# Reordering the loads of a two-problem attention kernel: fifth chunk's tokens earlier, weight blocks at a shorter lead, the second problem's tokens sooner

## The chip, the cores and the metric

One core of a Trainium2 chip. The metric is device time in microseconds (us) of one execution.

## The reference

Two independent problems, A and B, of the same shape; each is a grouped-query attention block with cached keys and values, and the two outputs are put side by side.

```python
B, Sq, D = 16, 32, 1024                # x: 512 tokens of 1024, bf16
Hq, Hkv, Sk, Dh = 32, 4, 512, 128      # 32 heads on 4 cached key/value heads
q = (x @ wq)                           # wq: 1024 x 4096
scores = einsum("bhqd,bhkd->bhqk", q, k) * Dh ** -0.5
p = softmax(scores)
o = einsum("bhqk,bhkd->bhqd", p, v)
out = o.reshape(B, Sq, Hq * Dh) @ wo   # wo: 4096 x 1024
# result: concatenate([A's out, B's out], axis=-1)
```

## The kernel before

The tokens of a problem are needed with the model dimension on the partitions, in eight chunks of 128 ("token chunks" below). A's first four chunks are transposed on TensorE, the others by transposing DMAs. The projection of A's first eight heads is done chunk by chunk (`first_heads`), with the weights in eight pieces (`load_w0`). Everything later is a software pipeline of 128 slots, one for each pair of batch and key/value head: a slot does four matmuls of 256 columns for scores, four for values, and seven matmuls of 512 columns (six in every fourth slot) out of one long stream: the remaining heads of A's projection, B's projection, A's output, B's output.

```python
# start: order of the loads, all issued by SyncE [cut: tokens and weights of the first four chunks]
load_w0(0, HC, NF, REP)              # HC = 4
load_w0(HC, HC + 2, 0, REP)          # weights of chunks 4 and 5, 512 KB
load_x_transposed(HC)                # tokens of chunks 4 and 5
load_w0(HC + 2, DC, 0, REP)          # weights of chunks 6 and 7
load_x_transposed(HC + 2)            # tokens of chunks 6 and 7
load_wq(0, 2)                        # third weight block (heads 8 to 11), 1 MB
load_k(0); load_wq(0, 3); load_k(1); load_v(0); load_k(2); load_wq(0, 4); load_v(1)
# ... [cut]
first_heads(range(NF, REP), range(HC))
first_heads(range(REP), range(HC, DC - 2))    # chunks 4, 5: the first that need DMA-transposed tokens
# ... [cut: chunks 6, 7, and the copies out of PSUM]

def stream():                                 # [cut: output projections]
    for h in range(REP, HQ):
        yield from q_units(0, h)              # eight matmuls of 512 columns per head
    for h in range(HQ):
        yield from q_units(1, h)

units = stream()
run(units, 5)

plan = {}
def at(slot, fn, *args):
    plan.setdefault(slot, []).append((fn, args))

for j in range(2, 2 * NG // GRP):             # NG = 64, GRP = 4
    if j > 2:
        at(GRP * (j - 1) - 2, load_k, j)      # four transposing DMAs for A, one for B
    at(GRP * (j - 1) + 2, load_v, j, 2 if j < 3 else 1)
for c4 in range(5, 16):                       # weight blocks of four heads, 1 MB each
    need = (c4 - 2) * 4 * DC / 7.0
    at(max(0, int(need) - 10), load_wq, c4 // 8, c4 % 8)
for n, (d0, d1) in enumerate(((0, 2), (2, 5), (5, DC))):
    at(GRP * (n + 4) - 2, load_xT_b, d0, d1)  # B's tokens, transposing DMAs
# ... [cut: output weights]

for i in range(total_slots + LAG):
    if live:
        do_loads(i)
        scores(i)
    run(units, 1)
    # ... [cut: sums, values(i - LAG), normalize]
    run(units, 5)
    # ...
    run(units, 1 - (i % 4 == 3))
```

`do_loads(i)` does not tie a load to the time of slot `i`. It puts the load into SyncE's instruction list at that place; SyncE works through the list in order. In the trace of before, B's last tokens, put at slot 22, whose scores began at 70.5 us, were issued at 79.7; and the waits of SyncE that its view shows up to 110 us, after 0.7 us at the start, are 3.1 us, all for TensorE to free buffers. So a slot number is a place in a queue.

A caution on names: the block of heads 8 to 11 is called the third weight block (`c4` = 2, counted from one), but "fifth" to "ninth" weight block are `c4` = 5 to 9 of the loop, counted from zero. `c4` = 8 is B's first block.

## Time and profile before

| | before |
|---|---|
| time, median of the first three runs | 343.88 us (343.65 to 345.03) |
| span of the profiled execution (344.67 us) | 342.9 us |
| TensorE listed busy | 338.1 us |
| seven 512-column and eight 256-column matmuls (one slot), start to start | 2.38 us |
| granted TensorE clock, mean | 1.000 |

The page of the kernel before: busy time of the engines with the share of the span, and the chain of waits that ended last by engine.

```profile
PE 338.1 (99%) x2128; PEld 214.3 (63%) x2128; DVE 266.4 (78%) x336; ACT 186.1 (54%) x209; POOL 47.0 (14%) x206
...
PE 92%; DMA 4%; SPq 3%; issue 0%; ACT 0%; ACTq 0%
```

Listed busy time of TensorE says little, since matmuls overlap in this trace: a 512-column matmul is listed with 379 ns, but seven of them start within 1.51 us, 216 ns apart. So the question is whether the starts are ever further apart than that. The timeline of TensorE of the kernel before (start, length, instruction, count, and in brackets the idle time before it and who ended it):

```profile
7.60 5.17 PE L532 MATMUL q_ps<-xT,w_sb 128*128 128x512 bf16 x22
13.34 7.07 PE L532 MATMUL q_ps<-xT,w_sb 128*128 128x512 bf16 x32 [0.57 <-DMA xT<-in_A_x_dram]
...
85.47 0.59 PE L302 MATMUL q_ps<-xT,wq_sb 128*128 128x512 bf16 x2
86.22 1.02 PE L302 MATMUL q_ps<-xT,wq_sb 128*128 128x512 bf16 x4 [0.16 <-DMA xT<-in_B_x_dram]
```

There are two gaps in brackets: the first projection waits for the tokens of chunks 4 and 5, and B's projection, five matmuls in, waits for B's last tokens. The chain of waits shows when these DMAs were issued (start, length):

```profile
5.85 7.45 DMA xT<-in_A_x_dram
13.34 7.07 PE q_ps L532 x32
...
79.71 6.47 DMA xT<-in_B_x_dram
86.22 1.02 PE q_ps L302 x4
```

One more number matters for the argument: the third weight block, the first that the stream needs. Its DMA in the view of the weight tile, to 13 us:

```profile
L246 SPq DMA_DIRECT2D wq_sb<-in_A_wq_dram x1: 582/582/582, 12.3 to 12.3; - x1
...
DMA to landing us min/median/max: 7.7/7.7/7.7
```

It was issued at 12.3 and landed at 20.0 us. The stream's first matmul started at 20.24. Landing times below are computed in this way, as issue plus time to landing. By the packed traces of before and of the changed kernel, the 167 DMAs that SyncE issued landed in the order of their issue, in both.

### The profile page before, as it was taken

What the parts mean: (1) busy time and instruction counts of PE and PEld (TensorE: products, weight loads), DVE (VectorE), ACT (ScalarE), POOL (GpSimd) and SP (SyncE); (2) the same over time, 40 slices, a digit from 0 to 9 for tenths busy, and PEclk for the clock granted to TensorE, in tenths of its full rate; (3) what the DMA queues carried; (4) which work ended last, traced back from release to release, by engine and by line L of the source; (5) the groups of instructions that cost most, each with busy time, mean ns of one, the idle gap of its engine ahead of it and who ended that gap; (6) DMA issues with size and microseconds to landing.
All of it is one profiled execution on the core that took longest, in us unless ns stands there. A gap on an engine that the chain in (4) does not pass through costs nothing.

```text
span 342.9 us, 5510 instructions
## 1 busy us (share of the span) xinstructions
PE 338.1 (99%) x2128; PEld 214.3 (63%) x2128; DVE 266.4 (78%) x336; ACT 186.1 (54%) x209; POOL 47.0 (14%) x206
## 2 busy tenths in 40 slices
PE   8999999999999999999999999999999999999996
PEld 7356666666666666666666666666666666666555
DVE  1057988888888888988888889888988888888540
ACT  3067666666676666766655455555455455555010
POOL 0001111100111111111101212221122110111100
PEclk9999999999999999999999999999999999999999
DMA  6998999999999999989999557998449996530001
GB/s 177 284 229 185 353 244 277 234 188 231 248 280 276 267 261 232 228 243 280 269 332 289 138 124 190 273 331 221 118 118 298 337 188 139 113 103 0 17 17 33
DMA packets 127086, 71.70 MB, mean 209 GB/s; under 512 B 75857, under 2 KB 126289, under 8 KB 127057
## 3 DMA queue, kind: packets, MB, share of 16 engines
q1 hardware_dynamic: 126528, 70.21, 85.4%
q0 software_dynamic: 384, 1.05, 0.9%
q8 instruction: 17, 0.28, 0.4%
q14 instruction: 13, 0.10, 0.1%
q10 hardware_dynamic: 144, 0.07, 0.1%
HBM read 50.86 MB, written 2.10 MB: 154 GB/s over the span
## 4 chain that ended last, share of the span: by engine, by line
PE 92%; DMA 4%; SPq 3%; issue 0%; ACT 0%; ACTq 0%
PE f_ps L321 32%; PE q_ps L302 26%; PE s_ps L358 16%; PE ob L426 16%; DMA xT<-in_A_x_dram 2%; PE q_ps L532 2%; DMA xT<-in_B_x_dram 2%; SPq L276 1%; SPq L478 1%; SPq L466 0%; SPq L246 0%; ACT o_sb L330 0%; SPq L287 0%; SPq L705 0%; ACTq L330 0%
## 5 line engine op out<-in xcount | busy, mean ns | idle before, releaser
L366 ACT ACTIVATE p_sb<-s_ps,shift 128x1024 bf16<-128x1024 f32 x128 | 142.7, 1115 | 100.0 <-PE s_ps L358 87.5
L377 DVE TRANSPOSE_TENSOR_REDUCE parts<-p_sb 128x32 f32<-128x1024 bf16 x128 | 158.9, 1241 | 19.8 <-ACT p_sb L366 18.3
L321 PE MATMUL f_ps<-wo_sb,oT 128*128 128x512 bf16 (+1 forms) x544 | 131.8, 366 | 0.0
L302 PE MATMUL q_ps<-xT,wq_sb 128*128 128x512 bf16 x448 | 117.7, 379 | 0.2 <-DMA xT<-in_B_x_dram 0.2
L426 PE MATMUL ob<-p_sb,v_sb 128*128 128x256 bf16 x512 | 76.8, 273 | 0.0
L358 PE MATMUL s_ps<-qT,kT 128*128 128x256 bf16 x512 | 76.8, 273 | 0.0
L321 PEld LDWEIGHTS <-oT 128*128 128x128 bf16 x544 | 53.2, 98 | 36.0
L358 PEld LDWEIGHTS <-kT 128*128 128x128 bf16 x512 | 56.8, 113 | 28.4 <-issue 0.3
L302 PEld LDWEIGHTS <-wq_sb 128*128 128x128 bf16 x448 | 43.8, 98 | 31.9 <-issue 0.4
L426 PEld LDWEIGHTS <-v_sb 128*128 128x128 bf16 x512 | 50.1, 98 | 20.0
L448 DVE TENSOR_TENSOR oT<-r,ob 128x512 bf16<-128x512 f32 x64 | 44.0, 688 | 22.5 <-PE ob L426 22.0
L412 DVE STREAM_TRANSPOSE r<-rall 128x512 f32<-128x512 f32 x64 | 44.3, 691 | 1.1
L310 ACT CAST qT<-q_ps 128x512 bf16<-128x512 f32 x56 | 32.7, 583 | 14.1 <-PE q_ps L302 14.1
L395 POOL COPY half<-cs 64x32 f32<-64x32 f32 x32 | 6.6, 206 | 228.7 <-DVE cs L385 228.7
L330 ACT CAST o_sb<-f_ps 128x512 bf16<-128x512 f32 (+1 forms) x17 | 9.5, 559 | 24.4 <-PE f_ps L321 16.7
L532 PE MATMUL q_ps<-xT,w_sb 128*128 128x512 bf16 (+1 forms) x70 | 15.2, 368 | 0.6 <-DMA xT<-in_A_x_dram 0.6
L385 DVE TENSOR_REDUCE cs<-parts 128x32 f32<-128x128 f32 x32 | 12.0, 376 | 1.1
L532 PEld LDWEIGHTS <-w_sb 128*128 128x128 bf16 x70 | 6.8, 100 | 7.8 <-issue 0.9
L407 DVE RECIPROCAL rall<-sums 128x32 f32<-128x32 f32 x32 | 10.4, 325 | 1.6 <-POOL sums L404 1.6
L560 DVE CAST qT<-q_ps 128x512 bf16<-128x512 f32 x4 | 2.8, 692 | 10.4 <-PE q_ps L532 10.3
L332 POOL DMA_DIRECT2D out_dram<-o_sb x8 | 4.6, 575 | 33.1 <-ACT o_sb L330 33.1
L396 POOL TENSOR_TENSOR half<-half,cs 64x32 f32<-64x32 f32 x32 | 7.8, 244 | 2.6
(25 smaller groups left out, 47.0 us busy)
## 6 DMA issues: line engine op xcount, KB each, us to landing
wq_sb<-in_B_wq_dram SPq DMA_DIRECT2D x8, 1024.0 KB, 6.0
wo_sb<-in_A_wo_dram SPq DMA_DIRECT2D x8, 1024.0 KB, 6.3
v_sb<-in_B_v_cache_dram SPq DMA_DIRECT2D x16, 512.0 KB, 4.4
wo_sb<-in_B_wo_dram SPq DMA_DIRECT2D x8, 1024.0 KB, 8.1
v_sb<-in_A_v_cache_dram SPq DMA_DIRECT2D x15, 512.0 KB, 6.4
wq_sb<-in_A_wq_dram SPq DMA_DIRECT2D x6, 1024.0 KB, 6.1
w_sb<-in_A_wq_dram SPq DMA_DIRECT2D x2, 512.0 KB, 7.0
kT<-in_A_k_cache_dram SPq DMA_TRANSPOSE x64, 4.5
```

What stands on the lines that cost most here:

```text
L302: nc.tensor.matmul(ps[:], lhsT=w[:, dc, (h % 4) * DH:(h % 4 + 1) * DH], rhs=xT[pr][:, dc, :], start=(dc == 0), stop=(dc == DC - 1),)
L310: nc.scalar.copy(out=qT[pr, g][:, :, hl, :], in_=ps[:].rearrange("p (b s) -> p b s", s=SQ),)
L321: nc.tensor.matmul(ps[:, 0:width], lhsT=oT[pr, tt][:, h, :], rhs=wo_tiles[pr, nh, h // REP][:, h % REP, off:off + width], start=(h == 0), ...
L358: nc.tensor.matmul(s_ps[:, c, :], lhsT=kT[:, i % GRP, c, :], rhs=qT[pr, g][:, b, :, :].rearrange("p h s -> p (h s)"), start=True, stop=True,)
L366: nc.scalar.activation(out=p_sb[:], in_=s_ps[:], func=ACTF.Exp, bias=shift[:], scale=SCALE)
L377: nc.vector.tensor_reduce(out=parts[k][:, q, :, :].rearrange("p c h -> p (c h)"), in_=st[i]["p"][:].rearrange("p c (h s) -> p (c h) s", s=SQ),
L385: nc.vector.tensor_reduce(out=cs[:], in_=parts.pop(k)[:].rearrange("p q c h -> p q h c"), axis=AX.X, op=ALU.add,)
L407: nc.vector.reciprocal(out=rall[:, k, :], in_=quad.pop(k)[:])
L412: nc.vector.transpose(out=r[:].rearrange("p n s -> p (n s)"), in_=rall[:, k, o * 2 * REP:(o + 1) * 2 * REP] .unsqueeze(2).to_broadcast([P, ...
L426: nc.tensor.matmul(ob[j][:, q, :], lhsT=v_sb[:, i % GRP, c, :], rhs=st[i]["p"][:, c, :], start=(c == 0), stop=(c == KC - 1),)
L448: nc.vector.tensor_tensor(out=out, in0=rcp.pop(j)[:].rearrange("p (q h) s -> p q h s", h=REP), in1=ob.pop(j)[:].rearrange("p q (h s) -> p ...
L532: nc.tensor.matmul(first_q[h][:, ts], lhsT=w0[dc // HC][:, dc % HC, h * DH:(h + 1) * DH], rhs=xT[0][:, dc, ts], start=(dc == 0 and t0 == 0 ...
```

## The change

The intent: tokens of chunks 4 and 5 should not queue behind the weights of chunk 5; weight blocks should not push the keys, values and B's tokens back by arriving long before they are needed; B's tokens should come sooner. The rate of the stream in the formula is corrected to 6.75 matmuls a slot. A split adds a DMA, and loading the third values in one piece removes one.

```diff
-            load_w0(HC, HC + 2, 0, REP)
+            load_w0(HC, HC + 1, 0, REP)
             load_x_transposed(HC)
+            load_w0(HC + 1, HC + 2, 0, REP)
             load_w0(HC + 2, DC, 0, REP)
@@
-                at(GRP * (j - 1) + 2, load_v, j, 2 if j < 3 else 1)
+                at(GRP * (j - 1) + 2, load_v, j)
             for c4 in range(5, 16):
-                need = (c4 - 2) * 4 * DC / 7.0
-                at(max(0, int(need) - 10), load_wq, c4 // 8, c4 % 8)
+                need = ((c4 - 2) * 4 * DC - 5) / 6.75
+                at(max(0, int(need) - 7), load_wq, c4 // 8, c4 % 8)
@@
-                at(GRP * (n + 4) - 2, load_xT_b, d0, d1)
+                at(GRP * (n + 3) - 2, load_xT_b, d0, d1)
```

(The diff is cut; the rest of it is `load_v` without its pieces.)

More of the change, by code (lines that the diff above doesn't have):

```diff
@@ L280, in load_k, with load_v @@
                     )
-            def load_v(j, pieces=1):
+            def load_v(j):
                 v_sb = v_tiles[j] = kv.tile([P, GRP, KC, DH], BF16, name="v_sb")
-                v = kv_part(j, 2).rearrange("q (p c) d -> p q c d", c=KC)
-                for k in range(pieces):
-                    qs = slice(k * GRP // pieces, (k + 1) * GRP // pieces)
-                    nc.sync.dma_start(out=v_sb[:, qs], in_=v[:, qs])
+                nc.sync.dma_start(
+                    out=v_sb[:],
+                    in_=kv_part(j, 2).rearrange("q (p c) d -> p q c d", c=KC),
+                )
             xT = [None, None]
```

## The prediction

> **What bounds it now.** TensorE: the busy table gives PE 338.1 of 342.9 us, the chain of waits is 92% PE, granted clock 1.00. Busy time is a poor witness, as matmuls overlap ([...]here a 512-column matmul is listed with 379 ns), so I use the pitch of starts: in the timeline seven 512-column matmuls take 1.51 us (0.216 each), four 256-column ones 0.44; one slot (seven and eight of these) is 2.38 us, and from 20 us on slots follow at that pitch. The chain shows two places where data is missed after the first blocks:
> 1. 13.34 us: the first projection waits for transposed tokens of chunks 4 and 5 (idle 0.57 us; in pitch about 0.7). Issued at 5.85, landed 13.25, behind 512 KB of weights of chunks 4 and 5.
> 2. 86.22 us: B's sixth token chunk, issued at 79.71, landed 86.2 (idle 0.16; in pitch about 0.3).
>
> **What the change does.** No instruction on PE, DVE or ACT changes, only the order on SyncE's DMA queue. One weight load is split in two, one values load merged.
> - Tokens 4/5 have 256 KB less ahead. [...] At the 300 GB/s of 8 to 10 us (windows) that is 0.85 us (estimate): landing near 12.4, so wait 1 shrinks below 0.2. Chunk 5's weights land near 13.3, needed 14.4.
> - But the gain meets the next load: the third weight block, issued at 12.31, landed at 20.0, and its first weights entered PE at 20.04. DMA is saturated from 5 to 20 us and the bytes ahead of that block are unchanged, so it lands at 20.0 again; PE arrives near 19.6 and waits 0.3 to 0.5. Net gain at the start: 0 to 0.3 us.
> - B's tokens, four slots (9.5 us) sooner: the last part lands near 77 to 79, needed 85.9. Wait 2 vanishes: 0.3 us.
> - Weight blocks: seven slots' lead (16.7 us) against 6 us (up to 10.2) from issue to landing. Estimated landing against need, from the queue's pace (7.3 us per A chunk): fifth block 47 to 48 against 50.8 (before: 43.2); sixth 57 to 60 against 61.2 (before 50.7); seventh 66 against 72.5; B's first 78 against 83.7. The sixth is tightest. No stall expected.
> - After about 110 us the queue waits for buffers PE frees, so nothing changes to the end.
>
> **Prediction.** 343.88 - 0.3 - 0.1 = about 343.5 us; 8 in 10: 342.7 to 344.4 (before's three runs alone spread 1.4 us). Faster by over 2%: 0.01; within 2%: 0.97; slower by over 2%: 0.02.
>
> **What would show each step.** Token transposes landing about 12.4, PE's gap before chunk 4 under 0.2 us; a new gap of about 0.4 us at 20 us before the first matmul of the streamed projection, for its weight block; no wait for B's tokens near 86; the sixth weight block landing before 61 us without a wait; the same pitch and tail (13.7 us of output matmuls) afterwards.
>
> **What would make it wrong.** That weight block landing before 20.0, so that the start gains the full 0.6; the DMA queue slower in 40 to 60 us, so that the fifth or sixth block comes late and PE stalls; or transposes next to weights behaving otherwise than bytes over rate.

## The result, and the profile after

| | before | changed |
|---|---|---|
| time, median of 6 runs each | 344.77 us (343.65 to 345.5) | 343.89 us (343.45 to 344.2) |
| ratio, 95% interval | | 0.9977 (0.9955 to 0.9999) |
| span of the profile | 342.9 us | 342.3 us |

Executions over 1.5% slower than the fastest of the same kernel are left out of the means. A ratio here is the mean time of one kernel's fast runs over that of the other's fast runs of the same rounds, so it is not quite the ratio of the medians. The time lies inside the predicted range, and the change is "the same" at 2%.

The page of the changed kernel:

```profile
PE 337.9 (99%) x2128; PEld 214.1 (63%) x2128; DVE 266.2 (78%) x336; ACT 185.9 (54%) x209; POOL 46.7 (14%) x206
...
PE 96%; DMA 1%; SPq 1%; ACT 0%; issue 0%; ACTq 0%
```

The timeline of TensorE of the changed kernel, and below it that of the weight loads into TensorE:

```profile
7.63 12.12 PE L533 MATMUL q_ps<-xT,w_sb 128*128 128x512 bf16 x54
19.97 1.25 PE L302 MATMUL q_ps<-xT,wq_sb 128*128 128x512 bf16 x5 [0.21 <-ACT qT L561]
...
85.21 1.46 PE L302 MATMUL q_ps<-xT,wq_sb 128*128 128x512 bf16 x6
```

```profile
8.35 10.91 PEld L533 LDWEIGHTS <-w_sb 128*128 128x128 bf16 x52 [0.62 <-DMA w_sb<-in_A_wq_dram]
19.96 0.76 PEld L302 LDWEIGHTS <-wq_sb 128*128 128x128 bf16 x5 [0.71 <-DMA wq_sb<-in_A_wq_dram]
```

Both gaps of before are gone: nothing waits for tokens in the first projection, and B's projection runs through at 85 us. (The 54 matmuls take 12.12 us where other profiles have 11.84: one waits 0.29 us at 8.35, for weights.) A new wait stands at 20 us: the weights of the stream's first matmul go in at 19.96, when the third weight block has landed. The 0.71 us in that row are idle time of the weight loads, which otherwise run ahead (in this packed trace a load starts 0.11 us before its matmul in the median, this one 0.004 us); of TensorE's own time 0.38 us are lost (its starts there are 0.59 us apart instead of 0.22). Its DMA:

```profile
L246 SPq DMA_DIRECT2D wq_sb<-in_A_wq_dram x1: 581/581/581, 10.6 to 10.6; - x1
...
DMA to landing us min/median/max: 9.4/9.4/9.4
```

It was issued 1.7 us sooner than before and landed at practically the same time, 20.0 (to the hundredth, 19.92 for 19.99). The tokens of chunks 4 and 5 landed at 11.4 for 13.3. B's last tokens landed at 72.6 (issued at 68.7) for 86.2. The fifth, sixth and seventh weight blocks landed at 47.3, 57.0 and 67.1, later than before (43.2, 50.7, 58.2), as predicted, and nothing waited for them.

So far the picture is the one that was predicted. But it is made of one profiled execution of each kernel, and a gap of 0.3 us in one profile need not be there in the next. The experiments therefore had to answer two things: which part of the change does what, and how steady the two gaps of before are.

### The profile page after: what moved, and what is told of

Its sections match the earlier page's. It is cut to its first block, busy times and chain, and to the rows that moved or that the text cites. A ratio compares the mean times of both kernels' runs of the same rounds, so it can differ in the third digit from the quotient of the medians.

```text
span 342.3 us, 5511 instructions
## 1 busy us (share of the span) xinstructions
PE 337.9 (99%) x2128; PEld 214.1 (63%) x2128; DVE 266.2 (78%) x336; ACT 185.9 (54%) x209; POOL 46.7 (14%) x206
## 4 chain that ended last, share of the span: by engine, by line
PE 96%; DMA 1%; SPq 1%; ACT 0%; issue 0%; ACTq 0%
PE f_ps L321 32%; PE q_ps L302 28%; PE ob L426 16%; PE s_ps L358 16%; PE q_ps L533 3%; DMA w_sb<-in_A_wq_dram 1%; SPq L478 0%; SPq L466 0%; ACT qT L561 0%; ACT o_sb L330 0%; SPq L706 0%; ACTq L330 0%
## 5 line engine op out<-in xcount | busy, mean ns | idle before, releaser
L377 DVE TRANSPOSE_TENSOR_REDUCE parts<-p_sb 128x32 f32<-128x1024 bf16 x128 | 158.8, 1241 | 20.0 <-ACT p_sb L366 18.3
```

The source lines that it names most:

```text
L377: nc.vector.tensor_reduce(out=parts[k][:, q, :, :].rearrange("p c h -> p (c h)"), in_=st[i]["p"][:].rearrange("p c (h s) -> p (c h) s", s=SQ),
```

## The experiments

All runs gave correct results. To compare profiles I cut the span into three: until the first matmul of the scores in slot 0 ("first scores"); from there to the start of the last copy out of PSUM ("the slots"); and from there to the end of the span ("the end"). Where nothing waits, the middle part came out as 318.23 or 318.24 us in nine profiles of seven different kernels, so that whatever it has above that is waiting. (Times in us, read from the timelines; "end" uses the span to the hundredth, from the packed trace; "wait" names what the timeline of TensorE shows after first scores.)

| profile | first scores | slots | end | span | wait in the slots |
|---|---|---|---|---|---|
| before | 21.32 | 318.55 | 3.01 | 342.9 | B's tokens |
| before, again (e8) | 20.98 | 318.23 | 3.02 | 342.2 | none |
| before, again (f4) | 20.45 | 320.22 | 3.01 | 343.7 | B's tokens |
| changed | 21.05 | 318.24 | 3.01 | 342.3 | none |
| changed, again (f1) | 20.27 | 318.23 | 3.01 | 341.5 | none |
| e1, start alone | 21.07 | 318.23 | 3.44 | 342.7 | none |
| e2, tokens alone | 21.00 | 318.23 | 3.01 | 342.2 | none |
| e3, lead alone | 20.91 | 318.23 | 3.08 | 342.2 | none |
| f2, changed without start | 20.79 | 318.23 | 3.07 | 342.1 | none |
| e4, half block | 20.79 | 319.06 | 3.44 | 343.3 | values |
| e7 and f3, interleaved | 20.29, 20.72 | 318.23, 318.23 | 3.44, 3.44 | 342.0, 342.4 | none |
| e5, lead of four | 20.78 | 319.70 | 3.01 | 343.5 | weights, B's keys |
| e6, tokens later | 20.41 | 329.74 | 3.01 | 353.2 | B's tokens |

### The parts one at a time: e1, e2, e3 (five rounds, one call)

e1, the kernel before with the reorder of the start only:

```diff
-            load_w0(HC, HC + 2, 0, REP)
+            load_w0(HC, HC + 1, 0, REP)
             load_x_transposed(HC)
+            load_w0(HC + 1, HC + 2, 0, REP)
```

> The kernel before with only the start reordered (fifth chunk's weights and tokens ahead of the sixth's weights). My theory: the 0.57 us wait of the first projection at 13.3 us is gone, the third weight block still lands near 20.0, so the weight load at 20 us waits about 0.7 us and the first scores start at 21.05 instead of 21.32: gain 0.25 to 0.3 us. B's tokens are still late: the PE idle of about 0.1 to 0.3 us near 86 us stays or grows by the 0.3 us that PE comes earlier, so that the net gain at the end is about 0, 0 to 0.3 us. Rival (the start alone carries the whole gain): 0.6 us or more at the end, no wait at 86.

Measured: 344.3 us, ratio 1.0000 (0.9985 to 1.0014). First scores at 21.07, as expected, and no matmul of the first projection waited. But the expected wait of 0.7 us at 20 us was not there either: TensorE itself came late in this execution (its long row of 512-column matmuls began at 8.32 us, for 7.60 in before; why, see e7 and f3). And B's last tokens, which this kernel loads as before does, landed at 84.5, and nothing waited near 86. This was the first sign that the gaps of before differ between executions.

e2, the kernel before with B's tokens four slots sooner only:

```diff
-                at(GRP * (n + 4) - 2, load_xT_b, d0, d1)
+                at(GRP * (n + 3) - 2, load_xT_b, d0, d1)
```

> The kernel before with only B's tokens asked for four slots sooner. My theory: no wait for B's tokens near 86 us, last part landing before 80; the wait of 0.57 us at 13.3 stays; gain 0.2 to 0.4 us over before. Rival (tokens sooner push weight blocks back into a new wait): a new PE wait between 45 and 100 us.

Measured: 343.84 us, ratio 0.9988 (0.9973 to 1.0002). B's last tokens landed at 77.4; no wait in the slots; the wait of 0.56 us for the tokens of chunks 4 and 5 stayed. And yet the first scores came at 21.00, no later than with the start reordered (21.05 and 21.07). The rival (a new wait) fell.

e3, the kernel before with the shorter lead (and the values in one piece) only:

```diff
-                need = (c4 - 2) * 4 * DC / 7.0
-                at(max(0, int(need) - 10), load_wq, c4 // 8, c4 % 8)
+                need = ((c4 - 2) * 4 * DC - 5) / 6.75
+                at(max(0, int(need) - 7), load_wq, c4 // 8, c4 % 8)
```

> The kernel before with only the weight blocks' lead (seven instead of ten, and the values load in one piece). My theory: the ninth weight block now stands behind the last part of B's tokens in the queue, not ahead of it, so that this alone also moves those tokens about 3 to 4 us sooner and the wait near 86 us is gone without their being asked for sooner: gain 0.2 to 0.4 us; weight blocks land later but no wait. The two changes are then each sufficient for that wait. Rival (the later blocks cost something): PE waits for a weight block between 45 and 100 us, time equal or worse than before.

Measured: 343.9 us, ratio 0.9993 (0.9979 to 1.0006). B's last tokens were issued at 74.6 and landed at 80.2, although they were not asked for sooner: the ninth weight block (1 MB) had stood ahead of them in the queue and now stood behind. No wait in the slots. So either part alone takes that wait away; in the changed kernel it is taken away twice. (The merge of the third values, which e3 holds too, was not run by itself; it saves one DMA, against the 1 MB block.)

### What binds the start after the change: e4

The changed kernel with the third weight block in two halves:

```diff
-            load_wq(0, 2)
+            load_wq(0, 2, parts=((0, 2), (2, 4)))
```

> The changed kernel with the third weight block loaded in two halves, first two heads first. My theory: after the change the start is bounded by that block's landing at 20.0 us; with the half of it landing near 18.8 the first streamed matmul starts near 19.6 to 19.7 instead of 19.97, first scores near 20.7 to 20.8, gain 0.3 us over the changed kernel unless the first keys (landing 20.4) bind. Rival (what binds at 19.97 is the copy of the seventh head out of PSUM, which ended at 19.95): the first streamed matmul stays at 19.97 and nothing is gained.

Measured: 344.6 us, ratio to before 1.0009 (0.9996 to 1.0023). The first half landed at 17.2. The stream's first matmul started at 19.48 instead of 19.97, right behind the first projection. The rival fell: the copy of ScalarE that the bracket in the changed kernel's timeline names ran here from 19.25 to 19.83 us, and the matmul did not wait for it. So in the profile of the changed kernel it had been the weight block; the bracket names what ended last by the profile, and there the copy (19.36 to 19.94) ended within some hundredths of a microsecond of the landing. But there was no gain. The timelines of TensorE, of the weight loads, and of TensorE again, of this run:

```profile
19.48 1.24 PE L302 MATMUL q_ps<-xT,wq_sb 128*128 128x512 bf16 x5
```

```profile
20.79 0.36 PEld L358 LDWEIGHTS <-kT 128*128 128x128 bf16 x4 [0.56 <-DMA kT<-in_A_k_cache_dram]
```

```profile
31.79 0.61 PE L426 MATMUL ob<-p_sb,v_sb 128*128 128x256 bf16 x4 [0.63 <-DMA v_sb<-in_A_v_cache_dram]
```

The second half's issue took SyncE 3.0 us instead of 0.58, the keys landed at 20.7 for 20.4, and the first values at 31.7 for 30.0, too late. Of the 0.49 us at 19.48, 0.26 were left at first scores, and 0.83 were lost at 31. The end, too, is 0.43 us longer than in the changed kernel, for a reason that has nothing to do with the block (last section on e7 and f3).

### How much room the shorter lead leaves: e5

```diff
-                at(max(0, int(need) - 7), load_wq, c4 // 8, c4 % 8)
+                at(max(0, int(need) - 4), load_wq, c4 // 8, c4 % 8)
```

> The changed kernel with weight blocks at four slots' lead instead of seven. My theory: the lead in slots acts only through the order of the SyncE queue, which runs late in the first 80 us; with four, the sixth block stands behind the fifth values and sixth keys, issues near 57 us, lands near 63, needed at 60.9: PE stalls about 2 us there, and perhaps 0 to 1.5 us more for the seventh. Total 2 to 4 us slower than the changed kernel (346 to 348). Rival (seven slots leave ample spare time, so four does too): no stall, 344.

Measured (3 rounds): 344.43 us median, but with a wide spread (343.47 to 346.33); ratio to before 1.0016 (0.9981 to 1.0052), which is unclear. The profile shows the mechanism that was expected. TensorE's timeline:

```profile
62.81 1.47 PE L302 MATMUL q_ps<-xT,wq_sb 128*128 128x512 bf16 x6 [0.91 <-DMA wq_sb<-in_A_wq_dram]
```

The sixth block was issued at 55.8, because it now stands behind the fifth values and sixth keys, and landed at 62.8. TensorE lost 1.08 us there and 0.38 at 188 us, for keys of B (the seventh block's weight load waited 0.28 us, which cost TensorE nothing). So the slots took 1.47 us above 318.23, less than the 2 to 4 expected; in two of the four executions (343.5 us) there can have been hardly any wait. So seven slots are enough and four are at the edge. In the changed kernel the sixth block landed at 57.0 for a first use at 62.0, 5 us ahead.

### The dose: B's tokens later, e6

The kernel before with the tokens four slots later than it has them:

```diff
-                at(GRP * (n + 4) - 2, load_xT_b, d0, d1)
+                at(GRP * (n + 5) - 2, load_xT_b, d0, d1)
```

> The kernel before with B's tokens four slots later than it has them (eight later than the change). My theory: the wait near 86 us is set by where the tokens stand in the queue: the last part then stands behind one more chunk of keys and values and one more weight block, issues near 86, lands near 92.5, needed 85.9: PE idle 6 to 7 us, total 350 to 351, nothing recovered afterwards. Rival (the wait near 86 in before is chance, tokens have spare time): about 344.

Measured (3 rounds): 354.18 us, ratio 1.0293 (1.0277 to 1.0309). The rival fell: the place in the queue decides. But the loss was larger than expected. TensorE's timeline, and the busy time in stretches around it (stretch, length, busy of PE, PEld, DVE, ACT, POOL, granted clock, DMA share, GB/s; the clock is what matters here):

```profile
84.78 0.38 PE L302 MATMUL q_ps<-xT,wq_sb 128*128 128x512 bf16 x1
93.96 1.86 PE L302 MATMUL q_ps<-xT,wq_sb 128*128 128x512 bf16 x4 [8.80 <-DMA xT<-in_B_x_dram]
95.61 1.06 PE L358 MATMUL s_ps<-qT,kT 128*128 128x256 bf16 x4
...
99.75 0.60 PE L358 MATMUL s_ps<-qT,kT 128*128 128x256 bf16 x4
```

```profile
85.00:90.00 5.00, 0.15 (x1) 0.00 (x0) 2.55 (x4) 0.22 (x1) 1.10 (x6) 0.89 0.73 165
90.00:94.00 4.00, 0.04 (x1) 0.04 (x1) 0.00 (x0) 0.00 (x0) 0.00 (x0) 0.50 1.14 314
94.00:95.00 1.00, 1.00 (x3) 0.36 (x3) 0.00 (x0) 0.00 (x0) 0.00 (x0) 0.50 1.76 323
...
98.00:99.00 1.00, 1.00 (x3) 0.29 (x2) 1.00 (x1) 0.00 (x0) 0.00 (x0) 0.50 0.52 92
99.00:100.00 1.00, 1.00 (x7) 0.60 (x6) 0.10 (x1) 0.05 (x1) 0.00 (x0) 0.91 0.87 287
```

Two terms make up the 11.5 us by which the slots exceed 318.23. The last tokens were issued at 87.1 and landed at 93.9 instead of 92.5, which TensorE waited for from 85.0 on: 9.0 us. The rest, 2.5 us, is the clock: the granted clock was 0.50 in every stretch from 90 to 99 us, so for the first 5.2 us of matmuls after the wait too (94.0 to about 99.2, from the share of 0.91 in the last stretch). The four 256-column matmuls at 95.61 took 0.86 us to the next row, the four at 99.75 0.44. So these 5.2 us lose half of that time, 2.6 us. The packed trace's record of the granted clock falls at 88.94 us, 3.9 us after TensorE began to wait, and returns at 99.18, 5.2 us after the first matmul; what sets these two moments was not shown. The wait of 2.0 us in f4 below (1.83 in its bracket) cost only itself: the clock there stayed 1.0 (1.00 from 84 to 92 us).

### The kernel before, again: e8 and f4

e8, one look, the same file:

> The kernel before once more, unchanged, for its profile. My theory: the wait near 86 us moves with the pace of the queue from one execution to another (in the run with the start alone the last tokens landed at 84.5 and nothing waited, in before at 86.2): here between 0 and 0.6 us; the first scores between 20.9 and 21.35. Rival (the waits are fixed): the same 0.3 us at 86 and first scores at 21.3.

Measured: 344.02 us (one run; its granted clock was 1.000). The timeline of TensorE, and that of its weight loads, in the unchanged kernel before:

```profile
7.93 11.84 PE L532 MATMUL q_ps<-xT,w_sb 128*128 128x512 bf16 x53
19.89 1.25 PE L302 MATMUL q_ps<-xT,wq_sb 128*128 128x512 bf16 x5
```

```profile
19.89 0.76 PEld L302 LDWEIGHTS <-wq_sb 128*128 128x128 bf16 x5 [0.62 <-DMA wq_sb<-in_A_wq_dram]
```

This is the profile of the changed kernel: no gap at 13 us, the wait for the third weight block at 20, nothing at 86 (B's last tokens were issued at 77.9 and landed at 84.3), a span of 342.2 us. Without one line of the change, both gaps that the prediction had set out to close were absent.

f4, five rounds of before against itself:

> The kernel before against itself: what the comparison calls a difference of nothing. Expected: a ratio of 1.000 with an interval of about 0.0015 to either side; in its profile a wait near 86 us between 0 and 0.6 us, first scores at 20.4 to 21.3.

Measured: 344.47 us, ratio 1.0003 (0.9986 to 1.0020); so an interval has a half-width of 0.0017, 0.6 us. In this profile the wait for B's tokens was larger than expected. TensorE's timeline:

```profile
84.60 0.59 PE L302 MATMUL q_ps<-xT,wq_sb 128*128 128x512 bf16 x2
87.02 1.02 PE L302 MATMUL q_ps<-xT,wq_sb 128*128 128x512 bf16 x4 [1.83 <-DMA xT<-in_B_x_dram]
```

TensorE came 0.87 us sooner than in the first profile of before (first scores at 20.45 for 21.32), and the tokens 0.8 later (87.0 for 86.2); the wait is what is between the two, so it grew to 2.0 us. With tokens and lead as in before, the four profiles (before, e1, e8, f4) have waits of 0.32, 0, 0 and 1.99 us there, 0.58 in the mean. With either part changed there was none for the tokens in any of nine (changed, f1, f2, e2, e3, e4, e5, e7, f3). The four come from different chips as far as the record says; chip and execution were not separated. But it is not the chip alone: in f4's call the profiled execution took 345.47 us, and the other four fast ones 344.19 to 344.52, so that these cannot all have had a wait of 2 us.

### Start or no start, and the changed kernel again: f1 and f2 (five rounds, one call with f3 and f4)

f1 is the changed kernel; f2 is the changed kernel without its reorder of the start:

```diff
-            load_w0(HC, HC + 1, 0, REP)
+            load_w0(HC, HC + 2, 0, REP)
             load_x_transposed(HC)
-            load_w0(HC + 1, HC + 2, 0, REP)
```

> The changed kernel once more. My theory, from the profiles so far: first scores near 21.0 as in most profiles of both kernels, third weight block landing near 20, no wait near 86; from first scores to the last copy out 318.2 us as in all runs without a wait; a ratio to before of 0.998 to 1.000. Rival (the change is worth a steady 0.6 us): first scores under 20.9 and a ratio of 0.998 or less with an interval clear of 1.

> The changed kernel with its reorder of the start undone (tokens' move and lead kept). My theory: the reorder of the start buys nothing, since the third weight block lands near 20 in any order: first scores at 20.4 to 21.3 as in before, no wait near 86, time within 0.3 us of the changed kernel in the same call. Rival (the start carries the gain): 0.3 to 0.6 us slower than the changed kernel.

Measured: f1 343.68 us, ratio to before 0.9989 (0.9972 to 1.0006); f2 344.0 us, 0.9993 (0.9976 to 1.0009). The two are 0.3 us apart in the median, which these intervals don't resolve. f1's profile contradicts my expectation of first scores near 21.0: they came at 20.27, the earliest of all, as the third weight block landed at 18.8 in that execution and nothing waited for it. Over all profiles with the block in one piece, first scores came at 20.84 us in the mean of seven with the old start (21.32, 21.00, 20.91, 20.98, 20.79, 20.45, 20.41) and at 20.79 in the mean of four with the new one (21.05, 21.07, 20.78, 20.27). The difference of 0.05 us is far inside the spread of nearly 1 us. Over the same profiles the third weight block landed at 19.52 in the mean with the old start (19.00 to 19.99) and at 19.49 with the new (18.82 to 19.92): the order of the loads did not move it. A part of the spread is not the loads at all, but the moment at which TensorE's clock rises (between 3.57 and 6.90 us in the 14 profiles, next section): a late TensorE finds its data there and waits less (in e1, whose long row began at 8.32 us, nothing waited at 20).

### A version meant to beat both: e7 and f3

The changed kernel with the third block in halves, the second half behind two key blocks, and the first values moved up:

```diff
-            load_wq(0, 2)
-            load_k(0)
+            load_wq(0, 2, parts=((0, 2),))
+            load_k(0, slice(0, 2))
+            # [second half of the block]
+            load_k(0, slice(2, GRP))
             load_wq(0, 3)
-            load_k(1)
+            load_k(1, slice(0, 2))
             load_v(0)
+            load_k(1, slice(2, GRP))
```

> The changed kernel with the third weight block in two halves, the second half behind the first two key blocks, and the first values between the second chunk's key blocks. In the run with halves alone the first streamed matmul came 0.49 us sooner (19.48 for 19.97), but the keys (20.7 for 20.4) and the first values (31.7 for 30.0) came late and cost 0.2 and 0.8 us. My theory: with those two moved up, first scores near 20.6 and no wait for values at 31: span about 0.4 us under the changed kernel (341.9), a ratio to before of 0.996 to 0.998. Rival (another load of the start then binds): first scores at 21 or a new wait before 45 us, no gain.

> The version with the split third weight block and values moved up once more, beside the changed kernel on the same chip. In its first profile the first scores came at 20.29 and nothing waited afterwards (318.23 us to the last copy), but 3.5 us passed from that copy to the end of the span, against 3.0 in most. My theory: first scores again near 20.3, 0.5 to 0.7 us before those of the changed kernel, and a median 0.3 to 0.7 us under it. Rival (the early start is given back at the end, or was chance): equal medians.

Measured: e7 343.82 us, ratio 1.0003 (0.9990 to 1.0017); f3 344.21 us, 1.0002 (0.9985 to 1.0020). It does not beat the changed kernel, and the hope was not borne out. The edit did what it was to do: the half landed at 18.3 and 17.7, nothing waited for it, and the slots ran in 318.23 us. Two things ate the gain. First, where the third block came at 18.8 anyway (f1), there was nothing to gain, and what decides then is when TensorE gets through the first chunks; the thirteen 256-column matmuls from 5.22 us on took 2.01 us in f1 and 2.46 in f3:

```profile
5.22 2.01 PE L533 MATMUL q_ps<-xT,w_sb 128*128 128x256 bf16 x13
```

```profile
5.22 2.46 PE L539 MATMUL q_ps<-xT,w_sb 128*128 128x256 bf16 x13
```

The 0.45 us between them are the whole difference of the two in first scores (20.27 and 20.72). The cause is the clock. The clock column of the views can't show it, as it has 1.00 for both kernels from 0 us on; but the starts of the matmuls can. In f3 those of 256 columns follow 0.21 us apart until 6.0 us and 0.11 from 6.2 on, in f1 0.11 from 5.2 on. The packed trace's own record of the granted clock begins at that moment, 6.18 in f3 and 5.07 in f1. In all 14 profiles it begins between 3.57 and 6.90 us; the latest is e1, whose long row began latest (8.32 us). So what looks like a kernel's slow start can be the clock, with up to 0.8 us between two profiles (7.51 in f1, 8.32 in e1), twice what the whole change is worth.

Second, the end. In e7 and f3 3.44 us passed from the start of the last copy to the end of the span, for 3.0 in most. The waits of SyncE in the last microseconds of f1 and of f3:

```profile
SPq L706 <- DMA out_dram<-o_sb: 2.0, 1, 2.0
SPq L706 <- PEq L679: 1.9, 1, 1.9
```

```profile
SPq L712 <- DMA out_dram<-o_sb: 4.3, 1, 4.3
```

In all 14 profiles the end goes with the number of DMAs that SyncE issues: 3.01 or 3.02 us where it is 167, that of before and of the change (eight profiles), 3.07 or 3.08 where it is one less (e3, f2), 3.43 or 3.44 where it is one more (e1, e4, e7, f3). The packed traces show why. The program gives its DMAs eight completion semaphores in turn (numbers 102 to 109 in before and in the changed kernel), and at the end SyncE checks the eight in a fixed order, 0.06 us each (in before 102 to 105 at 337.63, 337.69, 337.75 and 337.81 us, and 109, the last, at 341.92). The last output (issued by ScalarE) has landed 2.03 or 2.04 us after the start of the copy in every profile, and 0.93 us follow the last check in every one. What differs is its semaphore: with 167 DMAs it is the eighth, and one check follows the landing (0.04 us); with 166 the seventh (0.11); with 168 the first, so that SyncE stands at the first check until then and all eight follow (0.47). The 0.43 us between the first and the last case are the seven further checks. So it is the place in a round of eight that counts, and not that one DMA more is more work. This fits e1, the start alone, which gained nothing, though its ratio is too coarse to show it; and it gives the merged values load in the change a use that its author may not have had in mind: it makes up for the split.

## Why the prediction was right, point by point

- The time (343.5 us, 342.7 to 344.4) and "the same" held: 343.89 us. Of 12 runs of the changed kernel the mean is 343.82, of 42 fast runs of the kernel before 344.27; in the two calls that had both, the difference of the means is 0.8 and 0.6 us (f4's runs of before counted in). So the gain is of the order of 0.5 us, about 0.15%, and of the predicted size (0.4); the single ratios (0.9977 and 0.9989) have intervals that just exclude and just include 1.
- "Tokens 4/5 land near 12.4, wait 1 shrinks": they landed at 11.4 and the wait was gone. The estimate of what the 256 KB ahead of them cost was too small: 1.8 us for 0.85 in this pair of profiles, 1.3 in the mean of all (12.7 in seven with the old start, 11.4 in seven with the new). No profile with the new start has that wait; with the old one four of seven have it (before, e2, e3, f2), three not (e8, f4, e6).
- "The gain meets the next load; it lands at 20.0 again": shown for the profile of the changed kernel, which lost 0.38 us there, by e4, which moved that load and with it the start of the stream. It is not so in every execution: in f1, e1 and e5, with the same start, nothing waited at 20 us. The predicted net gain of 0 to 0.3 us at the start is 0.05 over eleven profiles, in effect zero. The DMA share that the prediction calls saturated was 1.11 in the mean of 5 to 20 us in before and 1.14 in the changed kernel, at 250 and 252 GB/s.
- "Wait 2 vanishes": yes, in nine profiles with one part or the other. The prediction took the two causes for one; e2 and e3 show that each alone is enough. The last tokens came sooner (72.6) than the estimate (77 to 79).
- "No stall from the shorter lead": right; the estimates for the fifth, seventh and B's first block (47 to 48, 66, 78) met the landings (47.3, 67.1, 77.7) within 1.1 us, and the sixth, 57.0, came at the early edge of its 57 to 60. That the queue waits after 110 us for buffers that TensorE frees holds: in before SyncE waited 49.8 us for TensorE from 110 to 336 us, against 3.1 up to 110.
- What the prediction did not see, though the time came out right: it read the two gaps of one profile as fixed costs of 0.7 and 0.3 us. They are not. The same kernel had neither in e8, and none at the first and 2.0 us at the second in f4. The step that was mis-sized is "Wait 2 vanishes: 0.3 us": it is 0 to 2 us, 0.58 in the mean of four profiles. What the change buys is mostly that B's tokens no longer meet TensorE by a hair. That the sum came so near was partly luck: the one profile that it was read from happened to hold a wait between those of the others.

Several of my expectations were wrong. In size: e6 lost 11.5 us in the slots for 6 to 7, as the clock came on top and the tokens landed 1.4 us later than estimated; e5 lost 1.5 for 2 to 4; f4's wait was 2.0 for at most 0.6. In kind: e1's wait at 20 us was not there, f1's first scores came 0.7 us sooner than I said, e4 was to gain 0.3 us over the changed kernel and came out slower, by the ratios to before, and the interleaved version was to gain 0.4 (e7) and to beat the changed kernel (f3), and did neither.

What stays open: whether the interleaved version would win with its DMA count made even, and what sets the landing of the third weight block between 18.8 and 20.0 us in one and the same kernel (the chip differed too).

## What to carry to other kernels

Where an in-order queue runs late, a load's "lead" is only its place in the queue: work out what stands ahead of it (in e5 the sixth block, behind one more load of values and one of keys, was issued at 55.8 us and landed at 62.8, for 57.0 in the changed kernel), and expect two edits that swap the same pair of loads to be worth one (e2 and e3 each left no wait for B's tokens). Before a gap of some tenths of a microsecond is treated as a cost, profile the unchanged kernel again, and look at the starts of its first matmuls for the moment of full clock (3.57 to 6.90 us here); a wait that is the difference of two drifting arrival times is worth its mean and its worst case, not the value in one trace (here 0 to 2.0 us, 0.58 in the mean of four). When a load is moved up, look at the next one that was within the same margin, for the gain stops there (here tokens that landed 1.8 us sooner, and 0.38 us lost at the third weight block).

## What the traces showed besides

- Issuing the transposing DMAs of 128 KB took long: four of them held SyncE for 5.1 us (26.7 to 31.7 us in before), about 1.3 us each, and for up to 8.6 us (from 11.2 us in the changed kernel). A plain DMA of the weights, whose issue took 0.58 us in the median of before, took 3.0 us in one place (e4).
- The landings keep the order of issue (167 of 167 in before and in the changed kernel), but their times vary: the third weight block of the changed kernel landed at 20.0 us in one execution and at 18.8 in another, B's last tokens of the kernel before at 84.3, 86.2 and 87.0.
- The moment of full clock at the start lies between 3.57 and 6.90 us in the 14 profiles, a range of 3.3 us, though the first matmul started at 0.93 us in each of the ten whose timelines were read from 0.
- The end of the span went with the completion semaphore that the last DMA got: 3.01 us with the last one checked, 3.44 with the first, in 14 profiles.
